# A transformer block on one core: a new order of all operations, and 49 unread products in TensorE's program

## The chip, the cores and the metric

The kernel runs on one core of a Trainium2 chip. The metric is the device time of one execution in microseconds (us), the median over runs.

## The reference

Four batches of 544 rows pass through three layers. The first is local and global attention in 8 heads of 64: 32 global rows see everything, 512 local rows see the global ones and neighbours within 32. The second is a gated mixture of four causal attention heads, two for each row. The third is a gated feed-forward layer with a convolution of width 3.

```python
# layer 1, per batch and head
s_g = scale * q_g @ k_all.T;  out_g = sm(s_g) @ v_all
s_l = concat(scale * q_l @ k_g.T, where(|i - j| <= 32, scale * q_l @ k_l.T, -1e9))
out_l = sm(s_l) @ concat(v_g, v_l)
# layer 2, x is 544 x 512 (32 global and 512 local rows, 8 heads of 64)
for e in range(4):
    ye = causal_softmax(scale * (x @ wq[e]) @ (x @ wk[e]).T) @ (x @ wv[e]) @ wo[e]
    out += (e among the two chosen) * w * ye
# layer 3
h = relu(x @ w_in)
conv = sum_k conv_w[k] * shifted(h, k - 1)
y = (h * sigmoid(conv)) @ w_out
```

## The kernel before

Every batch goes through three stages. Stage A is layer 1, two head pairs at a time: scores of the global rows (L648) and of the local rows with their masks (L575, L583), a maximum on VectorE (L586), exponentials on ScalarE (L592, L654, L656), transposes against an identity on TensorE (L599, L665), products with the values (L612, L675), a division, and transposes of the result (L629, L684) into activations that are held as a high and a low part. Stage B is layer 2: projections of queries and keys (L727) and values (L747), causal scores (L811), transposes (L838), products with the values (L857), and the same for the last 32 rows (L877 to L911). Stage C is layer 3, whose first weight has been folded with layer 2's output weight (L514): L940 makes h, VectorE, GpSimd and ScalarE make the gate, L982 the output. The big products take their fp32 operands as high and low parts, three products for each. The scores and value products of stage A work in tiles of 64x32 or 128x32 of the array, stage B's in 64x128 or 128x64; everything else uses the whole array, 128x128.

Nothing of the order is left to loops. Each stage calls `op()` once for every operation, a small group of instructions with an engine, a duration, what it reads and writes, and a priority: a place in the stage's stretch of the time plan (PLAN, SUB) plus a number of the operation's own (FINE, some 1,900 of them). `Schedule.run` then plays a timetable of the five engines, in which SP issues the loads and stores. At every step it looks, for each engine, at the operations whose inputs are ready and for which buffers are free, keeps those that can start within SLACK of the earliest one, and takes the one with the lowest priority; on TensorE an operation in another tile mode than the one before counts as HOLD later. An operation is passed over while its priority is more than HORIZON above that of the first operation not yet taken. Caps (CAPS) limit how many buffers of a kind live at a time. The timetable counts TensorE's instructions in blocks of 255 and adds a delay where a block would come late. The resulting list is what each engine's program holds, in that order; waits between engines follow from the tiles that are read and written.

TensorE starts with nine products of a cleared tile (L1024). PSUM has eight banks of 512 columns, `P_` in the code, which the operations take and give back as the timetable tells. GpSimd scales maxima (L372), normalises rows (L830) and copies gate logits (L752).

Of the kernel before, what the change touches and what calls it, by code (L numbers as in the profile page):

```python
# [8 lines left out]
F32 = mybir.dt.float32  # L9
# [131 lines left out]
class Op:  # L141

    __slots__ = ("eng", "dur", "fn", "prio", "mode", "size", "bufs", "succ", "wait", "ready", "n", "tag", "port")


class Schedule:
# [4 lines left out]
    SLACK = 0.092  # L151
    HOLD = 0.538
    HORIZON = 3714.57
    RATE = 415e3
    FETCH, BEHIND, AHEAD, COLD = 3.1, 1.75, 25, 4.0
# [8 lines left out]
    def op(self, eng, dur, fn, r=(), w=(), g=(), mode=None, size=0, lead=0.0, tag=""):  # L164
        o = Op()
        o.eng, o.dur, o.fn, o.mode, o.size, o.tag = eng, dur, fn, mode, size, tag
        o.tag = tag = f"{tag}@{self.batch}" if tag and self.batch else tag
        o.prio = self.prio - lead + self.FINE.get(len(self.ops), self.OFF.get(tag, self.OFF.get(tag.split("@")[0], 0.0)))
        o.port = "DVE" if eng == "POOL" else "POOL" if eng == "DVE" and tag.split("@")[0] in self.SHARED else None
        o.n = len(self.ops)  # L170
        o.succ, o.wait, o.ready = [], 0, 0.0
        before, bufs = {}, {}
        for t in r:
            wr, rd = self.last.setdefault(t, ([], []))
            before.update(dict.fromkeys(wr))
        for t in w:
            wr, rd = self.last.setdefault(t, ([], []))
            before.update(dict.fromkeys(wr))
            before.update(dict.fromkeys(rd))
        for t in g:  # L180
            wr, rd = self.last.setdefault(t, ([], []))
            before.update(dict.fromkeys(wr))
            before.update(dict.fromkeys(rd))
        for t in w:
            self.last[t] = ([o], [])
        for t in r:
            if t not in w:
                self.last[t][1].append(o)
        for t in tuple(r) + tuple(w):
            b = t[0] if isinstance(t, tuple) else t  # L190
            if isinstance(b, Buf):
                bufs[b] = 1
        o.bufs = tuple(bufs)
        for b in bufs:
            b.left += 1
        for p in before:
            p.succ.append(o)
            o.wait += 1
        self.ops.append(o)
        return o  # L200

    def run(self, trace=None):
        engines = ["PE", "ACT", "DVE", "POOL", "SP"]
        free = dict.fromkeys(engines, 0.0)
        avail = {e: [o for o in self.ops if o.wait == 0 and o.eng == e] for e in engines}
        order, mode, dma = [], None, 0.0
        port = {"DVE": 0.0, "POOL": 0.0}
        count, page, fetched, cold = 18, 189, 0.0, 0.0
        todo = sorted(self.ops, key=lambda o: o.prio)
        done, front = set(), 0  # L210
        left = len(self.ops)
        while left:
            while front < len(todo) and todo[front].n in done:
                front += 1
            limit = todo[front].prio + self.HORIZON
            pick = None
            for e in engines:
                cands = []
                now = free[e]
                for o in avail[e]:  # L220
                    if o.prio > limit:
                        continue
                    t, places = max(now, o.ready), []
                    for b in o.bufs:
                        if b.at is None:
                            f = b.space.find(b, t)
                            if f is None:
                                break
                            t = max(t, f[0] + 0.05)
                            places.append((b, f[1]))  # L230
                            b.space.take(b, f[1])
                    else:
                        cands.append((t, o, places))
                    for b, _ in places:
                        b.space.untake(b)
                if not cands:
                    continue
                m = min(c[0] for c in cands)

                def rank(c):  # L240
                    p = c[1].prio
                    if e == "PE" and c[1].mode != mode:
                        p += self.HOLD
                    return (p, c[1].n)

                c = min((c for c in cands if c[0] <= m + self.SLACK), key=rank)
                if pick is None or c[0] < pick[0]:
                    pick = c
            if pick is None:
                stuck = sorted((o for a in avail.values() for o in a), key=lambda o: o.prio)[:12]  # L250
                self.done = done
                raise RuntimeError("stuck: " + "; ".join(f"{o.eng} {o.tag} {o.prio:.0f}" for o in stuck))
            t, o, places = pick
            for b, at in places:
                b.space.take(b, at)
            if o.eng == "PE":
                span = o.dur + (self.SWITCH if o.mode != mode else 0.0)
                if free["PE"] > 0 and t - free["PE"] > 1.8:
                    cold = max(cold, t + self.COLD * min(1.0, (t - free["PE"] - 1.8) / 1.6))
                if cold > t:  # L260
                    span += min(span, (cold - t) / 2)
                end = t + span
                mode = o.mode
                while count + o.size > page:
                    at = end - span * (count + o.size - page) / o.size
                    stall = max(0.0, fetched - at)
                    if stall > 1.8:
                        cold = max(cold, at + stall + self.COLD * min(1.0, (stall - 1.8) / 1.6))
                    end += stall
                    ask = max(fetched, at + stall - self.AHEAD * span / o.size)  # L270
                    fetched = ask + self.FETCH + self.BEHIND * min(1.6, max(0.0, dma - ask) * self.RATE * 1e-6)
                    page += 255
                count += o.size
                free["PE"] = end
                end += self.TAIL["PE"]
            elif o.eng == "SP":
                free["SP"] = t + 0.45
                dma = max(dma, t + 1.6) + o.size / self.RATE
                end = dma + (0.9 if dma < 5 else 2.0)
            else:  # L280
                if o.port:
                    t = max(t, port[o.port])
                end = t + o.dur
                free[o.eng] = end - self.TAIL[o.eng]
                if o.port:
                    port[o.eng] = end
            if trace is not None:
                trace.append((o.eng, t, end, o.tag, o.prio, o.mode))
            order.append(o)
            done.add(o.n)  # L290
            left -= 1
            avail[o.eng].remove(o)
            for b in o.bufs:
                b.left -= 1
                b.end = max(b.end, end + self.LAT[o.eng])
                if b.left == 0:
                    b.space.release(b)
            for s in o.succ:
                s.ready = max(s.ready, end - self.TAIL["PE"] if s.eng == o.eng == "PE" else end + (0.03 if s.eng == o.eng else self.LAT[o.eng] + (0.04 if s.eng == "POOL" else 0.0)))
                s.wait -= 1  # L300
                if s.wait == 0:
                    avail[s.eng].append(s)
        self.span = max(free.values())
        return order
# [8 lines left out]


def t_pool(n, two=False):
    return (200 + (2.1 if two else 1.05) * n) * 1e-3


PLAN = {"A": [(-119.1, -47.3), (-21.7, 63.1), (38.1, 315.4), (307.0, 360.9)],
        "B": [(-137.7, -21.3), (148.2, 259.2), (249.9, 388.0), (376.3, 509.9)],  # L320
        "C": [(148.2, 401.7), (371.1, 480.9), (486.2, 654.7), (-670.0, 740.1)],
        "F": (162.2, -63.1),
        "U": (116.3, 210.9),
        "W": (-56.5, -20.9)}


CAPS = dict(raw=1, t=36, p=62, P=37, PT=2, PU=33, hb=44, cv=110, Pg=117, PGT=84)

MEM = (14, 11, 3, 4, 4)

# [6 lines left out]
def body(ctx, tc, kq, vA, wqv, woT, w_in, conv_w, w_out, cmask, out, trace=None,  # L337
# [31 lines left out]
    op = sch.op  # L369
# [651 lines left out]
    with tc.manual_schedule():  # L1021
        dve.memset(wz, 0.0)
        for k in range(9):
            pe.matmul(P_.view(7, 1), wz.bitcast(BF)[:, :128], wz.bitcast(BF)[:, 128:640], start=True, stop=True)  # L1024
# [71 lines left out]
```

## Time and profile before

| | |
|---|---|
| median of 3 runs | 422.12 us (421.61 to 422.59) |
| profiled execution, its own time | 423.22 us |
| its span, first to last instruction | 421.1 us |
| TensorE busy with products | 402.0 us (95%) |
| VectorE, ScalarE, GpSimd busy | 281.5, 253.1, 172.7 us |
| mean granted clock of TensorE | 0.986 |

In the profile, PE is TensorE's products and PEld its weight loads; each product has one weight load. L12 is line 12 of the kernel. A granted clock of 1.00 is 2.4 GHz, 0.50 is 1.2 GHz. Idle time of an engine is put down to what ended it: an instruction of another engine, a DMA, or "issue", when the profile shows nothing for which the engine waited.

### The profile page before, as it was taken

To read this page: it belongs to the slowest core of one execution; us is meant where nothing else is said; L and a number is where in the kernel's file an instruction comes from. 1 tells how busy PE (TensorE), PEld (TensorE's weight loads), DVE (VectorE), ACT (ScalarE), POOL (GpSimd) and SP (SyncE) were. 2 spreads that over 40 slices of the span, in tenths; PEclk is the share of its full clock that TensorE was granted. 3 is DMA by queue.
4 is the path that set the end of the run, shared out by engine and by line. 5 is a ranking of instruction groups with operands and counts; after the bars stand their busy time and mean duration, and the time that the engine had idled before them with its cause. 6 is when DMAs were issued, how large, how long until landed. Compare 5 with 4: busy or idle time off the path is not lost.

```text
span 421.1 us, 13314 instructions
## 1 busy us (share of the span) xinstructions
PE 402.0 (95%) x5605; PEld 362.5 (86%) x5605; DVE 281.5 (67%) x559; ACT 253.1 (60%) x616; POOL 172.7 (41%) x358
## 2 busy tenths in 40 slices
PE   7867899899899999999999999999999999999996
PEld 3656699677589999999889999899999999999996
DVE  2249858987787688886356558568675637758650
ACT  2866765765866746676476565675554556554531
POOL 3442563675775526460313232543331662262110
PEclk9888999999999999999999999999999999999999
DMA  8998922624523620233330200000000000000101
GB/s 309 396 345 299 339 98 75 215 90 147 184 82 107 207 97 2 89 125 125 120 127 0 94 5 2 28 29 2 2 2 2 26 28 29 29 0 28 54 26 54
DMA packets 15179, 42.34 MB, mean 101 GB/s; under 512 B 1552, under 2 KB 6416, under 8 KB 15120
## 3 DMA queue, kind: packets, MB, share of 16 engines
q1 hardware_dynamic: 15120, 41.49, 27.9%
q8 instruction: 44, 0.72, 0.7%
q14 instruction: 15, 0.12, 0.1%
HBM read 37.03 MB, written 4.46 MB: 99 GB/s over the span
## 4 chain that ended last, share of the span: by engine, by line
PE 84%; ACT 6%; DVE 4%; issue 3%; POOL 2%; DMA 1%; SPq 0%; ACTq 0%; DVEq 0%
PE acc L982 21%; PE acc L940 12%; PE acc L727 12%; PE acc L747 7%; PE acc L811 4%; PE acc L857 4%; PE acc L838 4%; PE acc L599 3%; PE acc L612 3%; PE acc L583 3%; ACT work L592 2%; PE acc L629 2%; DMA work<-in_w_out_dram 1%; PE acc L514 1%; PE acc L648 1%
## 5 line engine op out<-in xcount | busy, mean ns | idle before, releaser
L982 PE MATMUL acc<-xg,wuh 128*128 128x272 f32 x512 | 99.4, 292 | 0.0
L982 PEld LDWEIGHTS acc<-xg,wuh 128*128 128x128 f32 x512 | 79.9, 188 | 1.6 <-issue 1.2
L955 DVE SCALAR_TENSOR_TENSOR work<-work,cw 128x272 f32<-128x272 f32 x128 | 68.9, 560 | 18.2 <-POOL work L372 16.8
L982 PE MATMUL acc<-xg,wul 128*128 128x272 f32 x256 | 73.5, 287 | 0.0
L372 POOL TENSOR_SCALAR work<-work,cw 128x272 f32<-128x272 f32 x64 | 34.6, 551 | 53.3 <-ACT work L947 47.5
L940 PE MATMUL acc<-xg,wfh 128*128 128x274 f32 x256 | 51.6, 297 | 0.5 <-ACT work L667 0.5
L830 POOL TENSOR_SCALAR work<-work,st,gate 128x128 f32<-128x128 f32 (+3 forms) x64 | 46.5, 735 | 7.9 <-DVE st L827 6.1
L727 PE MATMUL acc<-xg,wqvh 128*128 128x272 f32 x256 | 49.7, 292 | 0.0
L982 PEld LDWEIGHTS acc<-xg,wul 128*128 128x128 f32 x256 | 48.2, 188 | 0.0
L592 ACT ACTIVATE work<-acc,st 128x128 f32<-128x128 f32 x128 | 37.1, 384 | 13.8 <-POOL st L372 13.7
L823 ACT ACTIVATE work<-acc,st 128x128 f32<-128x128 f32 (+3 forms) x64 | 33.1, 524 | 17.3 <-DVE st L816 12.0
L940 PEld LDWEIGHTS acc<-xg,wfh 128*128 128x128 f32 x256 | 40.2, 189 | 1.5 <-ACT work L667 0.8
L727 PEld LDWEIGHTS acc<-xg,wqvh 128*128 128x128 f32 x256 | 39.9, 188 | 0.9 <-issue 0.7
L940 PE MATMUL acc<-xg,wfl 128*128 128x274 f32 x128 | 37.1, 290 | 0.0
L727 PE MATMUL acc<-xg,wqvl 128*128 128x272 f32 x128 | 36.8, 287 | 0.0
L586 DVE TENSOR_REDUCE st<-acc 128x8 f32<-128x1024 f32 x16 | 19.5, 1219 | 22.6 <-PE acc L583 22.5
L947 ACT ACTIVATE work<-acc 128x546 f32<-128x546 f32 x32 | 20.0, 628 | 21.2 <-PE acc L940 17.6
L747 PE MATMUL acc<-wqvh,xg 128*128 128x260 f32 (+1 forms) x160 | 31.3, 286 | 0.0
L378 DVE TENSOR_TENSOR xg<-acc,xg 128x512 fp32r<-128x512 f32 (+3 forms) x56 | 22.6, 410 | 12.4 <-ACT xg L631 3.4
L840 ACT ACTIVATE work<-acc 128x512 f32<-128x512 f32 (+1 forms) x44 | 23.7, 558 | 11.3 <-PE acc L838 10.6
L378 DVE TENSOR_TENSOR xg<-work,xg 128x544 fp32r<-128x544 f32 x32 | 23.7, 744 | 9.4 <-ACT xg L964 8.6
L964 ACT ACTIVATE xg<-work 128x544 fp32r<-128x544 f32 x32 | 20.9, 659 | 13.8 <-DVE work L960 9.4
(138 smaller groups left out, 865.3 us busy)
## 6 DMA issues: line engine op xcount, KB each, us to landing
v<-in_vA_dram SPq DMA_DIRECT2D x32, 487.5 KB, 5.1
kq<-in_kq_dram SPq DMA_DIRECT2D x16, 624.0 KB, 5.2
work<-in_w_out_dram SPq DMA_DIRECT2D x8, 512.0 KB, 5.7
early<-in_w_in_dram SPq DMA_DIRECT2D x8, 512.0 KB, 6.8
out_dram<-work SPq DMA_DIRECT2D x15, 272.0 KB, 2.2
early<-in_wqv_dram SPq DMA_DIRECT2D x4, 386.0 KB, 8.8
early<-in_woT_dram SPq DMA_DIRECT2D x1, 512.0 KB, 9.0
out_dram<-work SPq DMA_DIRECT2D x2, 136.0 KB, 1.7
```

What stands on the lines that cost most here:

```text
L372: pool.tensor_scalar(dst, src, s, 1.0, op0=ALU.mult, op1=ALU.mult)
L378: dve.tensor_tensor(lo, src, hi.bitcast(F32), op=ALU.subtract)
L592: op("ACT", t_act(128, 1, 1), lambda y=y, t=t, sl=sl: act.activation(P[y].ap()[:, sl], S_(y)[:, sl], AF.Exp, bias=st.ap()[:, 8 + 4 * y + t ...
L727: pe.matmul(acc.ap()[:, 512 * z:512 * z + 272], wa[:, c, m], xa[:, s], start=(n == 0), stop=(n == 11))
L747: pe.matmul(acc.ap()[:r, :260], x[:, o_ + 128 * i:o_ + 128 * i + r], wa[:, c, :], start=(n == 0), stop=(n == 11))
L823: op("ACT", t_act(w, 1, 1) + .21, lambda tv=tv, st=st, y=y, k_=k_, Pb=Pb, c=c, h=h, w=w: act.activation(Pb.ap()[:, c:c + w], tv()[:, y, k_ ...
L830: op("POOL", t_pool(w), lambda Pb=Pb, st=st, c=c, h=h, e=e, w=w, i=i: pool.tensor_scalar(Pb.ap()[:, c:c + w], Pb.ap()[:, c:c + w], st.ap() ...
L840: op("ACT", t_act(128 * nb, 1), lambda PT=PT, tp=tp, nb=nb: act.activation(PT.ap()[:, :128 * nb], tp.ap()[:, :128 * nb], AF.Copy), r=[tp], ...
L940: pe.matmul(acc.ap()[:, 512 * f:512 * f + 274], a[:, p, sl], ov_(b)[:, x, p, 270 * z:270 * z + 274], start=(k == 0), stop=(k == 5))
L955: op("DVE", t_dve(272, 1), lambda hv=hv, cvv=cvv, f=f, F=F, z=z, k=k, o_=o_: dve.scalar_tensor_tensor(cvv()[:, f], hv()[:, f, o_:o_ + N], ...
L964: op("ACT", t_act(544), lambda G=G, cv=cv: act.activation(G.ap()[:, :544], cv.ap()[:, :544], AF.Copy), r=ct, w=[(G, 0)], tag="gh")
L982: pe.matmul(acc.ap()[:, 512 * m:512 * m + N], w[:, F, sl], G.ap()[:, o_ + N * f:o_ + N * f + N], start=(F == 0 and n == 0), stop=(F == 7 a ...
```

## The change

Four things change.

The order is another one. FINE and PLAN hold new numbers, nearly all of them; SUB and CAPS some; SLACK goes from 0.092 to 0, HOLD from 0.538 to 0.97, HORIZON from 3714.57 to 0.69, so that operations are taken nearly in the order of their priorities, on every engine. The operations themselves are the same.

Some durations in the timetable are others, nearly all of GpSimd: the memset of vB, the clipping of weights, the scaling of maxima, the copy of logits, the normalisation.

The timetable marks idle places of TensorE: where an operation of TensorE starts later than the engine and some bank are free, and before 130 us of the timetable, it puts down how many products of 0.22 us fit after 0.1 us. The bank is one that nobody owns, or one that the operation itself is about to write.

At these places the program gets that many products of the identity, seen as bf16, with itself, 128 by 128 weights and 512 columns. Their results are read by nobody. There are 49 of them at 17 places; each is a weight load and a matmul.

```diff
 class Schedule:
-    SLACK = 0.092
-    HOLD = 0.538
-    HORIZON = 3714.57
+    SLACK = 0.0
+    HOLD = 0.97
+    HORIZON = 0.69
     RATE = 415e3
+    WARM, SPARE = 130.0, 0.1
     FETCH, BEHIND, AHEAD, COLD = 3.1, 1.75, 25, 4.0
-    FINE = {0: -42.4, 1: 62.9, 2: 79.2, 3: 48.2,
...
+    FINE = {0: -19.0, 1: 99.2, 2: 109.9, 3: 110.1,
...
             if o.eng == "PE":
+                if 0 < free["PE"] and t < self.WARM:
+                    P = self.banks
+                    spare = [(max(P.free_at[i], free["PE"]), i) for i in range(P.count) if P.owner[i] is None or any(b.space is P and 0 <= i - at < b.n for b, at in places)]
+                    if spare:
+                        f, i = min(spare)
+                        n = int((t - f - self.SPARE) / 0.22)
+                        o.fill = [i] * n
                 span = o.dur + (self.SWITCH if o.mode != mode else 0.0)
...
-CAPS = dict(raw=1, t=36, p=62, P=37, PT=2, PU=33, hb=44, cv=110, Pg=117, PGT=84)
+CAPS = dict(raw=22, t=50, p=74, P=35, PT=13, PU=38, hb=19, cv=118, Pg=105, PGT=78)
...
-SUB = {"lk": -1.365, "lv": -20.969, "ly": -0.281, "lw": -129.791, "ag": 0.056, "az": 0.113, "bq": -0.039, "bp": 0.366, "bv0": -1.297,
+SUB = {"lk": 0.237, "lv": -18.39, "ly": -0.48, "lw": -130.134, "ag": 0.055, "az": 0.113, "bq": -0.04, "bp": 0.368, "bv0": -1.295,
...
-        op("POOL", 0.3, lambda: pool.memset(vB, 0.0), w=[("vB", i) for i in range(5)] + ["vBone", "vBraw"])
+        op("POOL", 1.2, lambda: pool.memset(vB, 0.0), w=[("vB", i) for i in range(5)] + ["vBone", "vBraw"])
...
+        half = ident.bitcast(BF)
         for o in order:
+            for i in o.fill:
+                pe.matmul(P_.view(i, 1), half[:, :128], half[:, None, :].to_broadcast([128, 2, 256]), start=True, stop=True)
             o.fn()
```

## Rows read from the trace of the kernel before

**Rows 1.** The page: busy us of the engines; the instruction queue's packets, MB.
```profile
PE 402.0 (95%) x5605; PEld 362.5 (86%) x5605; DVE 281.5 (67%) x559; ACT 253.1 (60%) x616; POOL 172.7 (41%) x358
...
q8 instruction: 44, 0.72, 0.7%
```

**Rows 2.** By stage: length, busy us of each engine, PE's clock, DMA share, GB/s.
```profile
0.00:130.00 130.00, 114.50 (x2048) 91.53 (x2050) 90.15 (x186) 85.75 (x219) 70.59 (x122) 0.96 0.60 213
130.00:417.84 287.84, 287.47 (x3559) 270.99 (x3557) 191.06 (x373) 167.04 (x396) 102.11 (x236) 1.00 0.15 50
```

**Rows 3.** PE's waits over the span: us in total, times, longest.
```profile
PE acc L583 <- issue: 3.3, 3, 1.6
PE acc L612 <- issue: 3.0, 1, 3.0
PE acc L599 <- ACT work L592: 2.5, 3, 1.5
...
PE acc L629 <- DVE work L621: 0.4, 1, 0.4
```

**Rows 4.** Busy time by stage in the three stretches of low clock.
```profile
10.27:13.68 3.41, 3.40 (x76) 2.64 (x76) 0.00 (x0) 2.87 (x8) 0.45 (x1) 0.50 1.03 409
23.92:27.33 3.41, 3.41 (x29) 2.99 (x28) 2.67 (x8) 1.88 (x6) 0.19 (x1) 0.50 0.95 329
37.57:40.99 3.42, 3.12 (x16) 2.71 (x15) 3.28 (x8) 1.74 (x5) 0.77 (x2) 0.50 0.53 212
```

**Rows 5.** Timeline of PE from 0 to 50 us: start, duration, instruction, idle before.
```profile
1.25 4.02 PE L1024 MATMUL acc<-vB 128*128 128x512 bf16 x9 [1.25 <-DVE vB L1022]
...
10.28 1.08 PE L599 MATMUL acc<-ident,work 128*128 128x128 f32 x4 [1.54 <-ACT work L592]
...
23.86 0.66 PE L612 MATMUL acc<-v,work 128*32 128x65 f32 x16 [2.96 <-issue]
...
24.72 1.92 PE L599 MATMUL acc<-ident,work 128*128 128x128 f32 x8
26.42 1.05 PE L629 MATMUL acc<-ident,work 128*128 128x128 f32 x4
...
31.48 0.66 PE L629 MATMUL acc<-ident,work 128*128 128x128 f32 x4
...
36.03 0.29 PE L583 MATMUL acc<-kq 64*32 64x128 f32 x1 [1.64 <-issue]
...
43.54 1.09 PE L599 MATMUL acc<-ident,work 128*128 128x128 f32 x8
...
48.67 0.84 PE L583 MATMUL acc<-kq 64*32 64x128 f32 x34 [1.45 <-issue]
```

**Rows 6.** By stage, from the start to the first and the last long stall.
```profile
0.00:20.88 20.88, 16.50 (x350) 9.98 (x351) 5.39 (x8) 11.63 (x32) 7.84 (x20) 0.92 0.94 353
...
0.00:47.30 47.30, 36.14 (x859) 25.13 (x859) 25.40 (x49) 30.33 (x78) 18.48 (x36) 0.89 0.92 333
```

**Rows 7.** The chain that ended last: start, us, what.
```profile
93.06 4.17 PE acc L514 x18
...
352.54 0.73 PE acc L811 x6
353.26 1.71 PE acc L940 x12
...
359.90 1.52 PE acc L940 x12
```

**Rows 8.** Groups by line: busy us, mean ns, idle before.
```profile
L840 ACT ACTIVATE work<-acc 128x512 f32<-128x512 f32 (+1 forms) x44 | 23.7, 558 | 11.3 <-PE acc L838 10.6
...
L583 PE MATMUL acc<-kq 64*32 64x128 f32 x1024 | 21.2, 286 | 3.3 <-issue 3.3
```

**Rows 9.** Busy time by stage where the loads end; last columns DMA share, GB/s.
```profile
50.00:52.00 2.00, 2.00 (x19) 2.00 (x18) 2.00 (x4) 0.81 (x2) 0.59 (x2) 1.00 1.04 420
54.00:56.00 2.00, 2.00 (x19) 2.00 (x18) 1.15 (x3) 2.00 (x7) 0.65 (x2) 1.00 0.26 102
```

More of the change, by code (lines that the diff above doesn't have):

```diff
@@ L141 @@
 class Op:
-    __slots__ = ("eng", "dur", "fn", "prio", "mode", "size", "bufs", "succ", "wait", "ready", "n", "tag", "port")
+    __slots__ = ("eng", "dur", "fn", "prio", "mode", "size", "bufs", "succ", "wait", "ready", "n", "tag", "port", "fill")
 class Schedule:
@@ L170, in op @@
         o.n = len(self.ops)
-        o.succ, o.wait, o.ready = [], 0, 0.0
+        o.succ, o.wait, o.ready, o.fill = [], 0, 0.0, ()
         before, bufs = {}, {}
@@ L316, in t_pool @@
     return (200 + (2.1 if two else 1.05) * n) * 1e-3
[L319 to L324, printed above, removed]
-CAPS = dict(raw=1, t=36, p=62, P=37, PT=2, PU=33, hb=44, cv=110, Pg=117, PGT=84)
+PLAN = {"A": [(-119.7, -48.2), (-21.9, 62.9), (38.1, 315.6), (307.4, 361.3)],
+        "B": [(-137.7, -21.3), (148.5, 259.4), (249.8, 388.0), (376.1, 509.8)],
+        "C": [(148.5, 401.8), (371.4, 481.1), (486.1, 655.3), (-668.3, 746.0)],
+        "F": (162.3, -62.8),
+        "U": (116.1, 210.9),
+        "W": (-52.9, -24.7)}
+CAPS = dict(raw=22, t=50, p=74, P=35, PT=13, PU=38, hb=19, cv=118, Pg=105, PGT=78)
 MEM = (14, 11, 3, 4, 4)
-SUB = {"lk": -1.365, "lv": -20.969, "ly": -0.281, "lw": -129.791, "ag": 0.056, "az": 0.113, "bq": -0.039, "bp": 0.366, "bv0": -1.297,
-       "bv": 0.609, "bg": 2.203, "b0": -0.896, "b1": 1.269, "b2": 1.01, "b3": 1.37, "bl": 1.25, "bs": 0.036, "ch": 0.098,
-       "co": 0.775, "cm": 0.686, "cf": -0.537, "cz": 0.902, "pi": 0.0, "pu": 0.0}
+SUB = {"lk": 0.237, "lv": -18.39, "ly": -0.48, "lw": -130.134, "ag": 0.055, "az": 0.113, "bq": -0.04, "bp": 0.368, "bv0": -1.295,
+       "bv": 0.609, "bg": 2.204, "b0": -0.896, "b1": 0.535, "b2": 1.01, "b3": 1.37, "bl": 1.249, "bs": 0.036, "ch": 0.098,
+       "co": 0.775, "cm": 0.684, "cf": -0.537, "cz": 0.902, "pi": 0.0, "pu": 0.0}
 @with_exitstack
@@ L363, in body @@
     P_ = Space(ps.tile([128, 4096], F32, name="acc"), 512, 8, None, 2)
+    sch.banks = P_
     W = lambda n=1, keep=0, group=None: Buf(W_, n, keep, group)
@@ L477, in decode @@
         op("ACT", t_act(n), lambda: act.activation(a(F32), u(F32), AF.Abs), r=rt + dz, w=[t], tag=tag)
-        op("POOL", t_pool(n), lambda: pool.tensor_scalar(a(F32), a(F32), MOST, LEAST, op0=ALU.min, op1=ALU.max), r=dz, w=[t], tag=tag)
+        op("POOL", t_pool(n) - .125, lambda: pool.tensor_scalar(a(F32), a(F32), MOST, LEAST, op0=ALU.min, op1=ALU.max), r=dz, w=[t], tag=tag)
         op("DVE", .45, lambda: dve.tensor_scalar(a(), a(), 3, 0x3FFFFFF8, op0=ALU.logical_shift_left, op1=ALU.bitwise_and),
@@ L587, in local @@
            r=[SS], w=[st], tag="maxA")
-        op("POOL", .25, lambda: scale_pool(st.ap()[:, 8:16], st.ap()[:, 0:8], 0.125), r=[st], w=[(st, 1)], tag="sclA")
+        op("POOL", .205, lambda: scale_pool(st.ap()[:, 8:16], st.ap()[:, 0:8], 0.125), r=[st], w=[(st, 1)], tag="sclA")
         for y in range(2):
@@ L652, in glob @@
         op("DVE", t_dve(544), lambda: dve.tensor_reduce(st.ap()[:, 0:1], G.ap()[:, 32:576], axis=AX.X, op=ALU.max, negate=True), r=[G], w=[st], tag="maxG")
-        op("POOL", .25, lambda: scale_pool(st.ap()[:, 1:2], st.ap()[:, 0:1], 0.125), r=[st], w=[(st, 1)], tag="sclG")
+        op("POOL", .19, lambda: scale_pool(st.ap()[:, 1:2], st.ap()[:, 0:1], 0.125), r=[st], w=[(st, 1)], tag="sclG")
         op("ACT", t_act(480, 1, 1), lambda: act.activation(Pg.ap()[:, :640].rearrange("p (n c) -> p n c", n=5)[:, :, 32:128],
@@ L751, in stage_b @@
                r=[acc], w=[("vB", i)], tag="vB")
-            op("POOL", .29, lambda i=i, r=r: pool.tensor_copy(lg[:r, i], vB[:r, i, :, 64]), r=[("vB", i)], w=[("lg", i)] + (["lg"] if i == 0 else []), tag="lg")
+            op("POOL", .19, lambda i=i, r=r: pool.tensor_copy(lg[:r, i], vB[:r, i, :, 64]), r=[("vB", i)], w=[("lg", i)] + (["lg"] if i == 0 else []), tag="lg")
         at("B", b, sub_["bg"])
@@ L829, in tiles @@
                     Pb, c, h, e = Ps[n // per], w * (n % per), y * np_ + k_, 2 * p + y
-                    op("POOL", t_pool(w), lambda Pb=Pb, st=st, c=c, h=h, e=e, w=w, i=i: pool.tensor_scalar(Pb.ap()[:, c:c + w], Pb.ap()[:, c:c + w], st.ap()[:, 12 + h:13 + h], gate[:, i, e:e + 1],
+                    op("POOL", .342 + .00084 * w, lambda Pb=Pb, st=st, c=c, h=h, e=e, w=w, i=i: pool.tensor_scalar(Pb.ap()[:, c:c + w], Pb.ap()[:, c:c + w], st.ap()[:, 12 + h:13 + h], gate[:, i, e:e + 1],
                        op0=ALU.mult, op1=ALU.mult), r=[(st, 4), gt], w=[(Pb, n % per)], tag="nrmB")
```

2 lines of the change are left out of this document (1 added, 1 removed).

## The prediction

> **What bounds the kernel now.** The page comes first: TensorE (PE) is busy for 402.0 of 421.1 us, VectorE, the next, for 281.5 [rows 1]. The table by stage then cuts the span in three: to 130 us PE is busy for 114.50 of 130.00 us, from there to its last product for 287.47 of 287.84 [rows 2], and 421.1 - 417.84 = 3.26 us remain for the last evictions and the last store. The reader is to see that after 130 us nothing is left but PE's own work, so that whatever PE loses or gains before 130 us reaches the end unchanged. The change can pay only in the 15.5 us of idle time before 130 us, in the clock there, and in the work itself.
>
> The list of PE's waits divides the idle time [rows 3]. Waits called "issue" make 3.3 + 3.0 = 6.3 us in four pieces; the first product waits 1.3 us for its operand. Six groups with waits of a third of a us and more, for results of ScalarE and VectorE, from L599's 2.5 us down to L629's 0.4, make 6.0 us in nine pieces. The rest, 15.5 - 6.3 - 1.3 - 6.0 = 1.9 us, is in small pieces.
>
> The clock is the other loss. In three stretches of 3.4 us the granted clock was 0.50, the lower level of 1.2 GHz, and PE worked there for 3.40 + 3.41 + 3.12 = 9.93 us [rows 4]. The same groups stand in the timeline at both levels: eight transposes of L599 took 1.92 us in such a stretch and 1.09 outside, four of L629 took 1.05 and 0.66 [rows 5]. That is 1.76 and 1.59 times, 1.67 in the mean, so the stretches cost about 9.93 x (1 - 1/1.67) = 4.0 us. The timeline's first row also has the first product's wait, 1.25 us. Before the first fall PE sat idle for 1.54 us, waiting for L592's exponentials; before the second it stood 2.96 us for "issue", before the third 1.64 us for "issue" [rows 5]. After the 1.45 us of "issue" that ended at 48.67 us no stretch followed.
>
> What "issue" is can be counted. Matmuls and weight loads before the first long one are 350 + 351 = 701, before the last 859 + 859 = 1718 [rows 6], 1017 apart or four blocks of 254; the one between them stands in the middle. The page has 44 packets in the instruction queue of 0.72 MB, and 11,210 instructions of PE over 44 are 255 too [rows 1]. So PE stood for its next block of instructions. All three stalls lie in groups of small products (L612 and L583) while the DMA engines were at their limit; the ends of the other blocks, most of them at a low DMA share, show no stall in [rows 3].
>
> **The change part by part.** *The ledger.* Before 130 us PE now loses 6.0 + 1.9 + 6.3 + 4.0 = 18.2 us (waits, small waits, blocks of instructions, clock), the start left out. I work out the same ledger for the new order.
>
> *The 49 products.* Each is a product of 128x512 in bf16. Nine of this shape took 4.02 us at the start, 0.447 each [rows 5]; eighteen fp32r products of the same size (L514) took 4.17 us later, 0.232 each [rows 7]. The first, 49 x 0.447 = 21.9 us, is the upper end. This form at the upper level does not stand in the trace; the diff's own 0.22 gives 10.8 us, and I take 0.232, the row at the clock that most of the 130 us had: 49 x 0.232 = 11.4 us. What hides them is the idle time they are put into. The rule in the diff puts int((gap - 0.1)/0.22) of them into each gap of its own timetable, so that 17 gaps add up to at least 49 x 0.22 + 17 x 0.1 = 12.5 us and at most 66 x 0.22 + 1.7 = 16.2. The trace of before has gaps of that size in nine places, with 6.0 us. So the new timetable has more of them, and the products make them real: where the chip would have had no gap, the product stands in front of ready work. Either way PE is taken for 11.4 us at these places, plus what the rule leaves, at least 0.1 each or 1.7 us; together 13.1 us instead of 6.0 + 1.9.
>
> *Their waits.* A product overwrites a bank, and so waits until the bank's last reader (ScalarE's or VectorE's eviction) is done. The rule picks the bank that is free first. If that eviction is late, the operation for which the gap was planned waits behind the product, and with it every later product of PE; then its evictions, and the operations that need those. I price this at nothing, since the gap's own releaser is usually later than the eviction; without this cover it is at most one eviction per place, 0.56 us for L840's of this size [rows 8], and 17 x 0.56 = 9.5 us.
>
> *Blocks of instructions.* 49 products are 98 more instructions, and the timetable does not count them for the blocks. Every block's end therefore falls up to 98 instructions earlier in the work than planned. Below lies 0 us (all ends fall into long products or into the filled gaps), above the 6.3 us of today. A new order with ends in new places gives no reason for either end; the 1718 instructions before the last stall hold six or seven block ends, four of which cost something, and stalls need dense small products and a full DMA together. I take a third, 2.1 us.
>
> The Trainium skill (Runtime: NRT & Kernel Launch, "Instruction fetch mechanics") says that the stream of instructions is fetched in blocks of 256 while the engine runs, and that crossing a block is mostly hidden. By that rule the forecast would be 2.1 us lower; the trace disagrees with it in the first 50 us, by 6.3 us, and agrees after that.
>
> *The clock.* The products keep PE at work in gaps for results, which preceded one of the three falls. They cannot run while PE has no instructions, which preceded the other two. Bounds: 0 to 4.0 us; with a third of the stalls left I take one stretch of three, 1.3 us.
>
> *The order.* All five engines get a new order, SP's loads among them, from priorities that are now followed within 0.69 of the first operation not yet taken. A group in another tile shape than the one before costs PE about 0.2 us: L940's twelve products took 1.71 us after a group of L811 and 1.52 us otherwise [rows 7]. With 16 groups each of L583 and L612 (1024 products by 64 [rows 8]) and a like number of others this is some 20 us in all, and the new rule prefers the same shape only within the 0.69. I see no sign of its direction: 0, with 10 changes of shape or 2 us to either side.
>
> *The timetable's durations* change no work. The cap on raw weight buffers rises from 1 to 22, so loads of w_out can start earlier; PE did not wait for them.
>
> *Sum.* New ledger: 11.4 + 1.7 + 2.1 + 1.3 = 16.5 us against 18.2, a gain of 1.7 us. The profiled execution took 423.22 us (its span 421.1 and 2.1 around it), 1.1 over the median of the three runs, 422.12. Taken off the median: **420.4 us**.
>
> **The rivals.** 0.2% is 0.84 us, about what a measurement of this kernel can tell from no change; so faster is under 421.3 and slower over 423.0.
>
> *All stalls and all slow stretches go.* The ledger is 13.1 us, the gain 5.1, the time 417.0. For it: all stalls and slow stretches lie in the first 50 us, and a search that counts blocks could lay their ends into long products. Against it: the 98 new instructions are not counted.
> The rule of the Trainium skill on instruction fetch, named above, would take the stalls' part of this rival as given; the 6.3 us in the trace keep its chance small.
>
> *The stalls stay (slower).* The first 50 us keep a full DMA (its share is 1.04 at 50 to 52 us and falls to 0.26 by 54 to 56 [rows 9]), and the moved block ends fall into L583, L612 or L648 again: 6.3 us, with one slow stretch. Ledger 13.1 + 6.3 + 1.3 = 20.7, 2.5 us more: 424.6. It decides as soon as stalls and clock together exceed 18.2 - 13.1 = 5.1 us.
>
> *More changes of tile shape (slower).* Fifteen more than now cost 3.0 us and end at 423.4; nine already eat the forecast's gain.
>
> *No change.* The weights for the projections (L727, L747), which begin behind the last long stall [rows 5], and the inputs for the groups before them come through a DMA that is full until 54 us. If that arrival sets the start of the unbroken work, stalls that go turn into gaps with products in them: 6.0 + 6.3 + 4.0 = 16.3 us now, against the 12.5 to 16.2 us planned. That gives 422.1, with products in the place of idle time.
>
> **How the numbers follow.** Forecast 0.40, all losses gone 0.15, together faster 0.55. No change 0.15. Stalls stay 0.22 and more changes of shape 0.08, together slower 0.30. The time is the forecast's, 420.4 us; its own range, by half a stall's sum and 10 changes of shape, is 418 to 423. The range for 8 in 10 takes in both outer cases, 417.0 and 424.6, and less than a us beyond: 416.2 to 425.2 us; what it leaves are a gain in changes of shape on top of all stalls, and late evictions in front of the products.
>
> **What would show it.** In the changed kernel's profile: 49 more products on a new line, in the first 130 us, with durations near 0.23 us apart; idle time of PE to 130 us of about 4 us instead of 15.5, of which "issue" about 2; one stretch at clock 0.50 after the first 10 us instead of three; PE still without a gap after 130 us. The step on the blocks is wrong if "issue" stays at 6 us or is gone; the step on the products is wrong if PE still idles 5 us at the places that they fill, or if products stand where their neighbours were ready. If the stretch from 130 us to the last product changes by more than 2 us, the order has changed the work's own length, and the ledger misses the cause.

## The result and the profile after

The changed kernel took 417.73 us in the median of 4 runs (416.50 to 417.87) against 421.93 (421.61 to 422.59): a ratio of 0.9892, 95% interval 0.9869 to 0.9915, 1.1% faster. The profiled execution took 417.87 us, its span 415.8. The time lies inside the range for 8 in 10 (416.2 to 425.2 us), just below the forecast's own range of 418 to 423, and 2.7 us below the forecast itself.

The page of the changed kernel, PE's busy time and the clock granted in 40 slices (to set beside [rows 1]):

```profile
PE 404.0 (97%) x5654; PEld 362.6 (87%) x5654; DVE 274.4 (66%) x561; ACT 250.0 (60%) x618; POOL 174.2 (42%) x358
...
PEclk9999999999999999999999999999999999999999
```

The same table by stage as in [rows 2]; the last product ends at 412.5 us, not at 417.84:

```profile
0.00:130.00 130.00, 123.71 (x2171) 97.86 (x2179) 93.89 (x193) 89.02 (x233) 71.30 (x124) 1.00 0.59 216
130.00:412.50 282.50, 280.29 (x3491) 264.79 (x3480) 180.23 (x368) 160.65 (x385) 102.87 (x235) 1.00 0.15 49
```

PE's idle time to 130 us is 6.29 us in place of 15.5, and there is no stretch at the lower clock. But behind 130 us, where before had 0.37 us of idle time, there are 2.21 us. The waits of PE over the span (us, times, longest; beside [rows 3]) say what they are:

```profile
PE acc L592 <- issue: 4.5, 4, 1.5
PE acc L1033 <- DVE vB L1031: 1.3, 1, 1.3
PE acc L621 <- issue: 0.6, 1, 0.6
PE acc L1037 <- ACT work L610: 0.5, 1, 0.5
PE acc L584 <- issue: 0.5, 1, 0.5
PE acc L684 <- DMA v<-in_vA_dram: 0.4, 1, 0.4
```

Stage A's lines have moved by nine (L583 is L592 now, L612 is L621), and L1037 is the unread products. "Issue" is 5.6 us, nearly what it was, and what is new is where. The timeline of PE (start, duration, instruction, idle before; beside [rows 5]):

```profile
1.25 3.51 PE L1033 MATMUL acc<-vB 128*128 128x512 bf16 x9 [1.25 <-DVE vB L1031]
...
6.20 1.25 PE L1037 MATMUL acc<-ident 128*128 128x512 bf16 x5
...
9.60 2.12 PE L1037 MATMUL acc<-ident 128*128 128x512 bf16 x9
11.65 0.41 PE L584 MATMUL acc<-cb 64*32 64x512 bf16 x8
...
13.36 0.67 PE L592 MATMUL acc<-kq 64*32 64x128 f32 x32 [0.85 <-issue]
...
31.84 0.66 PE L592 MATMUL acc<-kq 64*32 64x128 f32 x27 [1.53 <-issue]
...
44.31 0.47 PE L756 MATMUL acc<-wqvh,xg 128*128 128x260 f32 x1
...
205.95 0.38 PE L592 MATMUL acc<-kq 64*32 64x128 f32 x2 [1.25 <-issue]
...
255.56 0.65 PE L592 MATMUL acc<-kq 64*32 64x128 f32 x26 [0.84 <-issue]
```

The reader is to see three things. Nine products take 11.65 - 9.60 = 2.05 us, 0.228 each, so they stand back to back and their price is the one forecast. Two of the stalls, 1.25 and 0.84 us, lie far behind the loads, at 206 and 256 us. And the unbroken work of layer 2 (L756) begins at 44.31 us, 5.1 us earlier than in the kernel before (its first L747 began at 49.44 us, at the end of the group that the last stall had held up to 48.67 [rows 5]).

What stands before a stall called "issue" can be counted in every trace of this document. If TensorE's products, weight loads and its sequencer's own instructions are all counted from the start, the stalls of the changed kernel stand behind 449, 962, 1218, 1474, 6849 and 8385 instructions. Each of these numbers is a multiple of 256 plus 193 or 194. In the 14 traces there are 53 such stalls of more than 0.15 us, and every one stands at such a place. So these stalls come at the ends of blocks of 256 instructions; the 254 and 255 of the prediction are the same blocks, counted without the sequencer's own instructions.

### The profile page after: what moved, and what is told of

The parts are those of the page before. It is cut to its first block, busy times and chain, and to the rows that moved or that the text cites. A ratio compares the mean times of both kernels' runs of the same rounds, so it can differ in the third digit from the quotient of the medians.

```text
span 415.8 us, 13399 instructions
## 1 busy us (share of the span) xinstructions
PE 404.0 (97%) x5654; PEld 362.6 (87%) x5654; DVE 274.4 (66%) x561; ACT 250.0 (60%) x618; POOL 174.2 (42%) x358
## 4 chain that ended last, share of the span: by engine, by line
PE 88%; DMA 4%; DVE 3%; issue 2%; ACT 1%; SPq 1%; POOL 1%; POOLq 0%; DVEq 0%; ACTq 0%
PE acc L991 23%; PE acc L949 12%; PE acc L736 12%; PE acc L756 7%; PE acc L820 4%; DMA early<-in_wqv_dram 4%; PE acc L866 4%; PE acc L847 4%; PE acc L621 3%; PE acc L592 3%; PE acc L608 3%; PE acc L638 2%; PE acc L523 2%; PE acc L1037 2%; PE acc L886 1%
## 5 line engine op out<-in xcount | busy, mean ns | idle before, releaser
L964 DVE SCALAR_TENSOR_TENSOR work<-work,cw 128x272 f32<-128x272 f32 x128 | 63.9, 523 | 13.7 <-POOL work L381 12.8
L381 POOL TENSOR_SCALAR work<-work,cw 128x272 f32<-128x272 f32 x64 | 36.9, 584 | 53.1 <-ACT work L956 29.0
L839 POOL TENSOR_SCALAR work<-work,st,gate 128x128 f32<-128x128 f32 (+3 forms) x64 | 45.5, 717 | 11.3 <-DVE st L836 9.3
L601 ACT ACTIVATE work<-acc,st 128x128 f32<-128x128 f32 x128 | 36.9, 389 | 9.6 <-POOL st L381 9.0
L969 DVE SCALAR_TENSOR_TENSOR work<-work 128x544 f32<-128x544 f32 x32 | 23.7, 742 | 12.2 <-ACT work L968 12.0
L756 PE MATMUL acc<-wqvh,xg 128*128 128x260 f32 (+1 forms) x160 | 31.6, 287 | 0.0
L849 ACT ACTIVATE work<-acc 128x512 f32<-128x512 f32 (+1 forms) x44 | 23.1, 557 | 12.1 <-PE acc L847 11.4
L387 DVE TENSOR_TENSOR xg<-work,xg 128x544 fp32r<-128x544 f32 x32 | 24.6, 774 | 6.2 <-ACT xg L973 6.2
```

The costliest lines, as they stand in the source:

```text
L381: pool.tensor_scalar(dst, src, s, 1.0, op0=ALU.mult, op1=ALU.mult)
L387: dve.tensor_tensor(lo, src, hi.bitcast(F32), op=ALU.subtract)
L601: op("ACT", t_act(128, 1, 1), lambda y=y, t=t, sl=sl: act.activation(P[y].ap()[:, sl], S_(y)[:, sl], AF.Exp, bias=st.ap()[:, 8 + 4 * y + t ...
L756: pe.matmul(acc.ap()[:r, :260], x[:, o_ + 128 * i:o_ + 128 * i + r], wa[:, c, :], start=(n == 0), stop=(n == 11))
L839: op("POOL", .342 + .00084 * w, lambda Pb=Pb, st=st, c=c, h=h, e=e, w=w, i=i: pool.tensor_scalar(Pb.ap()[:, c:c + w], Pb.ap()[:, c:c + w], ...
L849: op("ACT", t_act(128 * nb, 1), lambda PT=PT, tp=tp, nb=nb: act.activation(PT.ap()[:, :128 * nb], tp.ap()[:, :128 * nb], AF.Copy), r=[tp], ...
```

## The experiments

Twelve kernels ran in three groups, each beside runs of before. The first group asks whether the gain is the order's or the products'. Its "before" was 421.30 us (23 runs).

**The order without the products.**

```diff
-            for i in o.fill:
+            for i in o.fill[:0]:
```

> The new order with the 49 products left out; nothing else is changed. Theory A (the products hold the clock, and that is the gain): stretches at granted clock 0.50 come back after the idle places, three or more before 45 us, each worth some 1.5 us, so 420 to 423 us. Theory B (the order makes the gain by itself, the products only fill what was idle): 417.5 to 418.5 us, the 11.4 us of the products turn into waits of the same length. Theory C (the products stand in the way of ready work): 414 to 416.5 us, PE's waits before 130 us are well under 11.4 us.

Measured: 415.63 us (6 runs, 413.95 to 417.09), ratio 0.986 (0.9824 to 0.9897). That is 2.1 us less than with the products. The six runs scatter by 3 us, but the changed kernel's medians, here and repeated below, are 417.73 and 418.00. Theory C's range holds the time, though not for C's reason: PE's idle time before 130 us came back almost whole, and so did one stretch at the lower clock (table by stage):

```profile
0.00:130.00 130.00, 114.87 (x2109) 93.50 (x2109) 93.03 (x191) 88.23 (x231) 71.29 (x123) 0.97 0.60 213
130.00:410.96 280.96, 280.85 (x3499) 265.58 (x3497) 181.46 (x370) 161.49 (x387) 103.04 (x235) 1.00 0.16 51
18.20:25.03 6.83, 4.58 (x80) 2.59 (x72) 1.55 (x6) 3.88 (x13) 4.78 (x5) 0.50 1.02 408
```

Its idle time to 130 us is 15.13 us, as in the kernel before (15.5). Behind 130 us there is 0.11 us and no stall. PE's timeline shows where the products had stood:

```profile
11.54 0.41 PE L584 MATMUL acc<-cb 64*32 64x512 bf16 x8 [2.05 <-ACT work L663]
...
17.45 1.33 PE L621 MATMUL acc<-v,work 128*32 128x65 f32 x64 [1.94 <-ACT work L610]
...
22.12 0.45 PE L684 MATMUL acc<-v,work 128*32 128x65 f32 x8 [1.67 <-issue]
...
45.89 0.39 PE L756 MATMUL acc<-wqvh,xg 128*128 128x260 f32 x1 [0.22 <-DVE xg L387]
```

The nine products that took 2.05 us stood in a wait of 2.05 us: these were free, but for the 0.1 us by which L584 started later (11.65 us for 11.54). At L756 the kernel without products is 45.89 - 44.31 = 1.58 us behind the one with them; at the last product it is 412.5 - 410.96 = 1.5 us ahead. So the products help up to 45 us, and then 3.1 us are lost again. Both kernels run the same products of the work in the same order, so their places in time can be set side by side. Here are a row before and a row behind each of the two late stalls, first without the 49 products:

```profile
203.14 1.53 PE L866 MATMUL acc<-work,vB 128*64 128x128 f32 x24
...
205.89 0.31 PE L756 MATMUL acc<-wqvh,xg 128*32 128x260 f32 x1
...
251.70 0.78 PE L684 MATMUL acc<-v,work 128*32 128x65 f32 x40
...
254.60 0.33 PE L693 MATMUL acc<-ident,work 128*128 128x128 f32 x1
```

The same four with the products:

```profile
201.89 1.53 PE L866 MATMUL acc<-work,vB 128*64 128x128 f32 x24
...
206.25 0.31 PE L756 MATMUL acc<-wqvh,xg 128*32 128x260 f32 x1
...
252.05 0.78 PE L684 MATMUL acc<-v,work 128*32 128x65 f32 x40
...
256.13 0.33 PE L693 MATMUL acc<-ident,work 128*128 128x128 f32 x1
```

The kernel with products is 1.25 us ahead before the first stall and 0.36 us behind after it, 0.35 us behind before the second and 1.53 us after it. So 1.61 + 1.18 = 2.8 of the 3.1 us go at these two block ends, and 0.3 us in all the rest.

**The products without the order.** The rule and the products were put into the kernel before; its own timetable marks 52 products at 18 places.

```diff
+                        n = int((t - f - self.SPARE) / 0.22)
+                        o.fill = [i] * n
...
+            for i in o.fill:
+                pe.matmul(P_.view(i, 1), half[:, :128], half[:, None, :].to_broadcast([128, 2, 256]), start=True, stop=True)
```

> The order of before with the same rule for products; its own timetable marks 18 places with 52 products. Theory A (clock): the first low stretch goes at least, the ones behind stalls may stay; 1.6 to 4 us less than before, 418 to 420.5 us. Theory B (order alone): no change, 421 to 423 us. Theory C (in the way): the trace of before had 6.0 us of idle time in places of that size, the products take 52 x 0.23 = 12 us, so up to 6 us more, 424 to 428 us, less what the clock gives back.

Measured: 421.19 us (12 runs, 420.11 to 423.22), ratio 1.0003 (0.9981 to 1.0025): no change, as theory B had it, and theory A's 418 to 420.5 us is missed. The clock was 1.00 throughout the work in the profile and the idle time to 130 us was 7.66 us in place of 15.5, so the products did what they are for. PE's busy time in the first stage is 122.34 us, 7.84 us more than before [rows 2], with 2138 - 9 - 52 = 2077 products of the work itself started against 2048 - 9 = 2039: little is won. By an estimate, the 52 products at 0.23 us are 12 us, of which 7.8 lie in idle time that is gone; the other 4 stood in front of ready work, as much as the clock costs by the prediction's estimate (4.0). The stage (busy us of each engine, clock, DMA):

```profile
0.00:130.00 130.00, 122.34 (x2138) 94.82 (x2139) 93.09 (x191) 87.93 (x225) 70.21 (x122) 1.00 0.59 215
```

**Every product twice.**

```diff
-            for i in o.fill:
+            for i in o.fill * 2:
```

> The new order with every product twice, 98 at the 17 places. It prices a product that stands in the way: 49 x 0.23 = 11.3 us more if the places have nothing left and nothing later takes it up, 429 us. If the start is set by the arrival of the loads, or the products stand behind something that is late anyway, the difference is well under half of that, 418 to 423 us.

Measured: 422.65 us (10 runs), ratio 1.0027 (1.0005 to 1.0049): 4.9 us over the 417.73 of the single products, for 49 more. That is 0.10 us for each in place of its 0.23, and not one effect but two. At the work that the changed kernel starts at 130 us the doubled one is 7.0 us behind, 0.14 us for each added product; the rest of the products went into idle time that was left (PE waits 3.5 us to 130 us, with the start, in place of 6.3). Then it gains 2.8 us back, because it has no stall at 206 and 256 us: its block ends have moved too.

**The first 14 products alone.**

```diff
-    WARM, SPARE = 130.0, 0.1
+    WARM, SPARE = 12.0, 0.1
```

> The new order with the products of the first two places alone (14, before 12 us of the timetable). Theory A: the clock stays up as far as these reach; idle places later let it fall again, once or twice, 418.5 to 421 us. Theory B: no change, 417.5 to 418.5 us. Theory C: the 35 products left out free PE where they stood in front of ready work, 414 to 417 us with the clock still up.

Measured: 414.59 us (4 runs, 414.04 to 414.81), ratio 0.9835 (0.980 to 0.987), the lowest median of all and 3.1 us below the changed kernel. From the order without any products (415.63, 413.95 to 417.09) the scatter does not separate it. The table by stage (length, busy us of each engine, PE's clock, DMA share, GB/s):

```profile
0.00:130.00 130.00, 118.89 (x2200) 95.92 (x2200) 94.63 (x193) 90.07 (x234) 72.22 (x124) 1.00 0.60 219
130.00:409.00 279.00, 278.80 (x3436) 263.85 (x3419) 180.31 (x367) 159.86 (x383) 101.65 (x235) 1.00 0.15 48
```

And PE's timeline, with the idle time before each row in brackets:

```profile
10.40 2.12 PE L1037 MATMUL acc<-ident 128*128 128x512 bf16 x9
...
17.43 1.11 PE L621 MATMUL acc<-v,work 128*32 128x65 f32 x64 [2.06 <-ACT work L610]
...
28.96 0.41 PE L584 MATMUL acc<-cb 64*32 64x512 bf16 x8 [1.29 <-ACT work L663]
...
31.70 0.45 PE L592 MATMUL acc<-kq 64*32 64x128 f32 x14 [1.50 <-issue]
```

The waits at 17 and 29 us are back, and the clock stayed at 1.00 through all of them in this execution (two of its four timed runs had a mean of 0.99 and 0.995). So here the other 35 products bring nothing that pays for them. That 14 hold the clock as well as 49 is not shown: with 14 products (this kernel and the one with its start cut, below) eight of ten runs had a mean clock of 0.996 or less, with 49 (the changed kernel, both times) one of ten.

The second group asks where the rest of the products' cost lies. Its "before" was 421.52 us (11 runs).

> The changed kernel once more, beside the others of this group. All theories: 417 to 418 us, two stalls called issue behind 130 us, 1.25 and 0.84 us.

Measured: the changed kernel again, 418.00 us (6 runs, 416.62 to 418.51), ratio 0.9916 (0.9883 to 0.9948), with stalls of 0.57 and 1.34 us behind 130 us, at the same two groups as in its first profile.

**The late products cut in four.** The 11 products behind 60 us keep their columns and become 44.

```diff
+            last = o.tag in ("scoresL", "transX@1", "transA@1", "pvA@1", "fold")
             for i in o.fill:
-                pe.matmul(P_.view(i, 1), half[:, :128], half[:, None, :].to_broadcast([128, 2, 256]), start=True, stop=True)
+                for k in range(4 if last else 1):
+                    if last:
+                        pe.matmul(P_.view(i, 1)[:, 128 * k:128 * k + 128], half[:, :128], half[:, :128], start=True, stop=True)
...
```

> The changed kernel with the 11 products behind 60 us each cut into four of 128 columns: the same columns, 66 more instructions. Theory D (the 98 instructions of the products move the ends of PE's instruction blocks, and the two stalls behind 130 us come from that): the ends behind 110 us move by another 66 instructions, the stalls at 206 and 256 us go, 2 us less, 415.5 to 416.5 us, unless other ends fall badly. Theory C (products in the way are the whole cost): no change, 417 to 418 us, or a little more.

Measured: 416.17 us (6 runs, 415.37 to 417.05), 1.8 us less than the same columns in fewer instructions; its ratio to before is 0.9877 (0.9845 to 0.9909). No wait is left behind 130 us; the stage (same columns) has 0.11 us of idle time:

```profile
130.00:411.44 281.44, 281.33 (x3505) 266.26 (x3503) 182.06 (x370) 162.37 (x390) 104.29 (x236) 1.00 0.15 51
```

More instructions made it faster, by moving the ends of the blocks: the ends at 6849 and 8385 instructions now fall elsewhere in the work. Theory D holds. (In this execution there was also one stretch at clock 0.50, at 32.81 us, so the 49 products do not hold the clock every time.)

**Products to 50 us.**

```diff
-    WARM, SPARE = 130.0, 0.1
+    WARM, SPARE = 50.0, 0.1
```

> The changed kernel without the 11 products behind 60 us, 38 products left. Theory C: the time at which PE reaches its later work falls by the 0.5 to 0.8 us that the late products cost; the stalls behind 130 us stay where they fall, 416.5 to 417.3 us. Theory D: 22 instructions fewer move the ends of the later blocks, the two stalls go or change, 413.5 to 415 us.

Measured: 416.39 us (6 runs, 415.26 to 417.86), ratio 0.9883 (0.9846 to 0.9919). One of the two late stalls went, one of 1.03 us stands at 254 us. It falls between the two theories: half of D's effect. The stall that stayed is again at 8385 instructions.

**Fourteen products, the start cut.**

```diff
-        for k in range(9):
-            pe.matmul(P_.view(7, 1), wz.bitcast(BF)[:, :128], wz.bitcast(BF)[:, 128:640], start=True, stop=True)
+        for k in range(18):
+            pe.matmul(P_.view(7, 1)[:, :256], wz.bitcast(BF)[:, :128], wz.bitcast(BF)[:, 128:384], start=True, stop=True)
```

> The new order with the 14 first products, and the nine products at the very start cut into 18 of half the columns: 18 more instructions at no time. It moves every block's end by 18 instructions. Theory D: the stalls called issue in the first 50 us (1.5 and 1.0 us with the 14 products alone) change in place and size, between none and 6 us; 412.5 to 418 us. If block ends do not matter, no change from the version with 14 products: 414.6 us within 0.5.

Measured: 415.50 us (6 runs, 414.14 to 417.52), ratio 0.9869 (0.9832 to 0.9905). The stalls moved as D says: 1.0 us is left in the first 50 us in place of 2.5, and one of 0.92 us is new at 253 us. The new one is at 8385 instructions too. The time did not fall, and the run had a low stretch again. The difference to 414.59 is within the scatter.

The third group tries the two suspects by themselves. Its "before" was 421.19 us (23 runs).

**Block ends alone, in the old order.** The start of the kernel before was cut in the same way, into 18 products and into 36; nothing else was changed.

> The kernel before with the nine products at its start cut into 18 of half the columns: 18 more instructions of PE at no time, which moves the end of every block of PE's instructions 18 instructions earlier in the work; nothing else is changed. Theory D (block ends in dense groups make the stalls called issue): their sum, 6.3 us in the trace of before, changes by 1 us or more to either side, and the time with it: 417 to 424 us. Theory E (the stalls come from the loads or from the order itself): the four stalls stay where they are, 421 to 422.5 us.

> The same with 36 products of a quarter of the columns, 54 more instructions. Theory D: other stalls again than with 18; 417 to 424 us. Theory E: as before, 421 to 422.5 us.

Measured: 419.16 us (12 runs, 418.66 to 421.08), ratio 0.9958 (0.9938 to 0.9978), and 419.66 us (12 runs), ratio 0.9969 (0.9952 to 0.9987). Both are faster than before, by nothing but 18 and 54 more instructions at the start. PE's longest waits with 18, beside [rows 3]:

```profile
PE acc L612 <- ACT work L601: 2.4, 2, 1.8
PE acc L599 <- ACT work L592: 2.2, 2, 1.6
PE acc L583 <- issue: 2.1, 2, 1.2
PE acc L629 <- ACT work L601: 1.8, 1, 1.8
```

"Issue" fell from 6.3 to 2.3 us with 18 (0.2 of it at L612) and to 2.1 with 36. But PE's idle time to 130 us is 130 - 114.59 = 15.4 us with 18, as in the kernel before: L612 and L629 now wait for ScalarE's copies (L601) where they had waited for instructions. In the two profiles the gain is the clock alone, which was not low in any stretch of the work with 18: the span fell by 421.1 - 416.8 = 4.3 us, and PE's busy time by 402.0 - 397.7 = 4.3. In the timed runs the clocks lie closer together (median 0.995 against 0.992), so how much of the 2.0 us there is the clock, and how much the stalls themselves, stays open.

**The price of a change of shape.** In the new order without products, 88 unread products of one column stand in front of big groups behind 150 us, once in the whole array and once in a tile of 128x32. The lines with a plus at the top are in both kernels; the last two are what differs between them.

```diff
+                if t > 150 and o.mode == mode == "f" and o.size == 24 and o.tag.split("@")[0] in ("h", "out", "projQK"):
...
+                        o.fill = [min(spare)[1]]
...
-                pe.matmul(P_.view(i, 1)[:, :1], half[:, :128], half[:, :1], start=True, stop=True)
+                pe.matmul(P_.view(i, 1)[:32, :1], half[:, :32], half[:, :1], start=True, stop=True)
```

> The new order without the 49 products; instead, behind 150 us, one unread product of a single column in front of each of 88 groups of 12 big products that follow work in the whole array, itself in the whole array, 128x128. Price of a product alone: 88 x 0.03 to 0.1 us, 2.6 to 9 us over the 415.6 us of the new order without products.

> The same 88 products of one column in a tile of 128x32, so that each makes two changes of tile shape. Theory S (a change of shape costs PE time, about 0.2 us for out and back as in the chain of before): 88 x 0.2 = 17.6 us more than the same products in the whole array. Rival: the 0.2 us belongs to the other groups and not to the change; within 4 us of it.

Measured: 426.59 us (4 runs) and 441.17 us (4 runs). The products alone cost (426.59 - 415.63) / 88 = 0.125 us each, more than was expected; that includes a stall of 0.96 us at 257 us, again at 8385 instructions. The tile adds 14.6 us, 0.166 us for each way out of the whole array and back, so theory S holds against its rival. (Between the two profiled executions it was 17.3 us, 0.20 each. Other tile shapes were not tried.) The rows of the products themselves hide it. The group of L1035 in the whole array (busy us, mean ns of one, idle before):

```profile
L1035 PE MATMUL acc<-ident 128*128 128x1 bf16 x88 | 15.4, 175 | 0.0
```

The same group in the tile, whose mean is only 2 ns longer:

```profile
L1035 PE MATMUL acc<-ident 128*32 128x1 bf16 x88 | 15.6, 177 | 0.0
```

## Why the prediction was right, and where it was not

**Direction and range** held; the gain was forecast as 1.7 us and measured as 4.2. The direction held in part by luck: what the forecast built its gain on, products in place of idle time, brought nothing in the old order (421.19 for 421.30 us) and cost 2.1 us in the new one, and the gain came from a term that it had set at 0. Two steps were wrong above all, the order and the block ends, and they partly cancelled. The prediction's own signs say so: "issue" stayed near 6 us (5.6), PE had gaps after 130 us (2.21 us), and the stretch from 130 us to the last product changed by more than 2 us (287.84 to 282.50, though it does not hold quite the same work).

**The order was set at 0, within 2 us. It was the whole gain.** Alone it brings 5.7 us (421.30 to 415.63). In the profiles, the last product ends 417.84 - 410.96 = 6.9 us earlier while the idle time to 130 us hardly changed (15.50 to 15.13); PE's busy time fell from 402.0 to 395.7. The forecast looked for the gain in idle time and found only room there. Of the 6.3 us of busy time three parts can be named. The work at the lower clock fell from 9.93 us [rows 4] to 4.58, which by the forecast's factor of 1.67 is worth 5.35 x 0.4 = 2.1 us. (In the timed runs the clocks differ less, 0.992 and 0.995 in the median, so this part is smaller there.) The products at the start took 0.3 us less. Changes of tile shape fell from 138 to 127, counted along PE's products; at 0.166 us for two of them that is 0.9 us.

So some 4 us of the 6.3, changes of shape included, are work that was shorter at the same clock. Two traces whose clock was low in no stretch of the work show nearly as much. PE is busy for 397.7 us in both, the old order with its start in 18 products and the new order with 14 unread products. Less the start (4.0 in both) and the 14 products (3.2), that is 393.7 us in the old order and 390.5 in the new. One more part of it can be read, but was not tested. The kernel before has 22 waits of PE above 0.15 us behind the start, the new order without products has 14; a product behind such a wait adds 0.34 us to PE's busy time in the mean, one in the middle of its group 0.06. By that estimate eight waits fewer are some 2 us, partly at the same places as the changes of shape. The rest, 1 to 2 us, stays open.

**A change of shape was mis-sized.** The forecast put 2 us on ten changes. Measured, ten changes are 0.8 us, and the 138 of before some 11 us, not 20.

**The products' price was right, their ledger was not.** They were forecast at 11.4 us: 49 x 0.228 = 11.2 by the nine in the timeline. The remaining waits were set at 1.7 us; the idle time to 130 us less the start (1.25) and the stalls (0.85 + 0.50 + 1.53 + 0.64 = 3.5) is 6.29 - 4.77 = 1.5. Wrong was the inference that 17 marked gaps mean a new order with more idle time than the 6.0 us of before. The old timetable marks 18 gaps and 52 products by the same rule, so it, too, shows far more than the chip had. A timetable's gaps cannot be set against a trace's. The order without products has 15.1 us of idle time, as before.

**The instruction blocks were set at 2.1 us and cost 5.6.** That PE stands for its next block was right, as the count of 256 shows, and it costs more than thought: 3.5 us before 50 us and 2.1 behind 200, where the forecast had seen no danger because before showed no stall there. Its condition that small products and a full DMA must come together was wrong; behind 60 us what goes with a stall is how fast the block before it ran. Of the 506 block ends behind 60 us in all traces, the 16 whose 256 instructions had run in less than 3.26 us hold all 11 stalls. By the split of the late products, 1.8 us of the changed kernel's time are these late stalls; set side by side with the order without products, 2.8 us. The Trainium skill's rule that a block's crossing is mostly hidden (Runtime: NRT & Kernel Launch, "Instruction fetch mechanics") would have made them nothing; the traces disagree.

**The clock was set at one low stretch and had none.** The products hold it in most executions: with 49, nine of ten runs had a mean of 0.998 or more, against a median of 0.992 before. At L756 the kernel with them is 1.6 us ahead of the one without. That this clock is worth its products in the end is shown by no run: the new order is slower with the 49 than without, and the old order with 52 products and a full clock is no faster than before.

**The rivals.** "All stalls and all slow stretches go" named the measured time, 417.0, for the wrong reasons: the slow stretches went, the stalls stayed. "The stalls stay" was right in its mechanism and wrong in its sum, since it, too, priced the order at nothing. "More changes of shape" went the other way. "No change" is what the products do without the order.

So the change is two opposite ones: an order worth 5.7 us, and products that gave back some 2 us of it. In the profiles they win 1.6 us up to 45 us and lose 3.1 after that, 2.8 of it at two block ends that their instructions moved into small products. That is a matter of where the count happens to fall, and not a price of the products' own time.

## What to carry to other kernels

Work put into idle time is free only where the idle time really is; try it with few products and with none, and look for what the added instructions move downstream. In a long straight-line program the count of instructions before a dense group is a parameter of its own: splitting hidden products moved this kernel by 0.4% with no other change. When an order is changed, weigh the time of the work itself (clock, changes of tile shape, neighbours), not the idle time alone.

## What the runs showed of the hardware

All 53 stalls called "issue" in these traces stand at the end of a block of 256 of TensorE's instructions, the sequencer's own counted. Such an end stopped TensorE for 1.25 us at 206 us, where the DMA share was 0.42 between 203 and 209 us, and for 0.84 us at 256 us, where it was 0.04 between 253 and 257; a full DMA is not needed for it. The 11 stalls behind 60 us all stand behind blocks that had run in 2.0 to 3.3 us. The granted clock stayed at 1.00 behind a wait of 2.06 us at 17.43 us in one execution with 14 products ahead of it, and went to 0.50 at 18.20 us behind waits of 2.05 and 1.94 us in one without them. A product of a single column in a stream of big ones cost 0.125 us, one stall counted in, though its row says 175 ns, and 0.166 us more when it used a tile of 128x32.
